# One tile of scores ahead of the last two chunks of values, with a buffer of its own for its exponents

## The chip, the cores and the metric

The kernel runs on one core of one Trainium2 chip. The metric is the time of one execution on the device in microseconds (us). The profile shows one execution; its span runs from the first to the last instruction of the program.

## The reference

Attention with pooled queries, then a small expert layer on 128 tokens of each batch. There are 8 batches, 8 heads, 1152 keys and values of 64 elements, and 576 pooled queries, all in fp32.

```
q_pool = q.reshape(B, H, S // 2, 2, D).mean(axis=3)
scores = scale * matmul(q_pool, k.T)            # scale = 1/sqrt(D)
attn   = exp(scores - max) / sum                # softmax over the keys
x      = matmul(attn, v), heads side by side    # (8, 576, 512)
for each batch b:
    top = the 128 rows with the highest x[b] @ w_gate
    out[b, top] = x[b, top] + sigmoid(score) * (relu(x[b, top] @ w1) @ w2)
```

## The kernel before

**Units of work.** Two heads make a pair; there are 32 pairs. The 576 queries of a pair are cut into two halves of 288, called s = 0 and s = 1, so the main loop in `run` goes over 64 halves, h = 0 to 63. The 1152 keys are cut into 9 chunks of 128 (NC = 9).

**Scores.** For every chunk, `scores` takes a tile from `banks()` and runs four products of 64 by 64 by 288 into it (L887; the trace has eight matmul records for the four fp32 products). ScalarE then takes the exponent of the whole tile, 128 x 576, into the SBUF tile `p` (L894). `p` holds nine such units and has two buffers, so the exponents of half h go where those of half h-2 were.

**Values.** `weighted` multiplies the exponents with the values, nine chunks one after the other, all summed in one tile of `banks()`, called `av` (L905). ScalarE copies that tile to `two` (L913), GpSimd adds its two planes (L915), and VectorE transposes the sum (L984).

**The order in a round of the loop.** In round h the program issues: the nine score tiles of half h and their exponents, small ScalarE copies for sums of earlier halves (L956 or L971), pieces of the expert layer that are due ("mid"), the sums of the exponents of half h (`folded`: three additions on GpSimd, L926, and two transposing reductions on VectorE, L931), the preparation of the next pair's keys and queries (`prepare_pair`, only where s = 0), the values of half h-1 and their copy `two`, and at the end more pieces of the expert layer. Every engine works through its instructions in this order.

**PSUM.** All matmul outputs come from one pool of four tiles, each of two banks:

```
self.psum = pool("psum", 4, space=psum)
def banks(self):
    return self.psum.tile([P, 2, 512], F32, name="ps")
```

The tiles are given out in turn. A request takes the tile given out four requests earlier and waits until its reader on ScalarE is done with it. Between two halves without a piece of the expert layer, the requests in order are: nine score tiles of half h, `av` of half h-1, nine score tiles of half h+1, and so on.

**Keys and queries of the next pair.** `load_pair` issues the transfers of keys and queries on SP's queue (L750, L756). `prepare_pair` adds neighbouring queries on GpSimd (`qp`, L775), transposes the keys on VectorE (`kT`, L778) and then the pooled queries (`qT`, L782). The scores of the next pair need both. The very first pair is prepared differently, with transposes on TensorE (`load_first`, `first_keys`, `first_queries`).

**Expert layer.** Batches are handled in twos by `layers_of_two`; its matmuls are L1362 with copies at L1370, and its activation is L1403. A search of the chosen rows runs on VectorE (L1201). What is left at the end is done in `ending` (L1439, L1449).

Semaphores are placed by the framework from the order of the program and what each instruction reads and writes. An instruction that waits for two engines has a separate EVENT_SEMAPHORE instruction ahead of it on its sequencer.

Of the kernel before, what the change touches and what calls it, by code (L numbers as in the profile page):

```python
# [10 lines left out]
P = 128  # L11
BLK = 32

G = 3
F32 = mybir.dt.float32
I32 = mybir.dt.int32
AF = mybir.ActivationFunctionType
ALU = mybir.AluOpType
# [14 lines left out]
def _any_scores(  # L33
# [451 lines left out]
    in_pair = [(j, t) for j in range(2) for t in range(NF)] + [(0, NF)]  # L485
    upcoming = load_pair(*pairs[0])
    run(prepare_pair(upcoming))
    preparing = iter(())
    routing = iter(())
# [50 lines left out]
class _Plain:  # L540
# [243 lines left out]
    def load_first(self, b, hp):  # L784


        nc, NC, D = self.nc, self.NC, self.D
        room = self.work.tile([P, self.NG, G, 2, self.HALF], F32, name="p")
        room = room.rearrange("p g u j n -> p (g u j n)")
        sixth, n_k = self.QB // 6, 2 * NC * D  # L790
        kn = room[:, 0:n_k].rearrange("p (c j d) -> p c j d", c=NC, j=2)
        n_q = 2 * 4 * sixth * D
        qn = room[0 : 3 * BLK, n_k : n_k + n_q].rearrange("p (a j m d) -> p a j m d", a=2, j=2, d=D)
        qp = room[0 : 3 * BLK, n_k + n_q : n_k + n_q + n_q // 2]
        qp = qp.rearrange("p (a n j d) -> p a n j d", a=2, j=2, d=D)
        v_sb = self.load.tile([P, 2, NC, D], F32, name="v_sb", bufs=2)
        heads = [2 * hp, 2 * hp + 1]
        of = self.q[b, 2 * hp : 2 * hp + 2].rearrange("j (i t m) d -> t i j (m d)", i=BLK, t=6)

        def queries(engine, half, groups):  # L800

            for g in groups:
                engine.dma_start(  # L803
                    qn[g * BLK : (g + 1) * BLK, half].rearrange("i j m d -> i j (m d)"), of[3 * half + g]
                )

        def keys(a, z):

            for j, h in enumerate(heads):
                rows = self.k[b, h].rearrange("(p c) d -> p c d", c=NC)  # L810
                nc.sync.dma_start(kn[:, a:z, j, :], rows[:, a:z, :])  # L811

        queries(nc.scalar, 0, (0, 1))
        queries(nc.sync, 0, (2,))
        for a in range(0, NC, G):
            keys(a, a + G)
        queries(nc.sync, 1, range(3))
        for j, h in enumerate(heads):
            of = self.v[b, h].rearrange("(p c) d -> p c d", c=NC)
            nc.sync.dma_start(v_sb[:, j, :, :], of)  # L820
        return {"k": kn, "q": qn, "qp": qp, "v": v_sb, "b": b, "hp": hp}
# [45 lines left out]
        self.first_keys(pair, 0, 1, self.nc.scalar.copy)  # L867
        self.first_keys(pair, 1, G, self.nc.vector.tensor_copy)

    def scores(self, half):  # L870

        nc, pair, n = self.nc, half["pair"], self.HALF
        qs = slice(half["s"] * n, (half["s"] + 1) * n)
        p = half["p"] = self.work.tile([P, self.NG, G, 2, n], F32, name="p")
        for c in range(self.NC):
            if "qp" in pair and half["s"] == 0:
                if c in (G - 1, G):
                    a = G * (c - G + 2)
                    self.first_keys(pair, a, a + G, nc.vector.tensor_copy)
                elif c == 2 * G - 1:  # L880
                    self.first_queries(pair, 1)
            sc = self.banks()
            for e in range(2):
                keys = slice(e * self.D, (e + 1) * self.D)
                for j in range(2):
                    rows = slice(j * self.D, (j + 1) * self.D)
                    nc.tensor.matmul(  # L887
                        sc[keys, j, 0:n],
                        lhsT=pair["kT"][rows, c * P + keys.start : c * P + keys.stop],
                        rhs=pair["qT"][rows, qs],  # L890
                        start=True,
                        stop=True,
                    )
            nc.scalar.activation(p[:, c // G, c % G, :, :], sc[:, :, 0:n], AF.Exp, scale=self.scale)  # L894

    def weighted(self, half):


        nc, n = self.nc, self.HALF
        av = self.banks()  # L900
        for c in range(self.NC):
            for e in range(2):
                keys = slice(e * self.D, (e + 1) * self.D)
                for j in range(2):
                    nc.tensor.matmul(  # L905
                        av[j * self.D : (j + 1) * self.D, e, 0:n],
                        lhsT=half["pair"]["v"][keys, j, c, :],
                        rhs=half["p"][keys, c // G, c % G, j, :],
                        start=(c == 0),
                        stop=(c == self.NC - 1),  # L910
                    )
        two = self.small.tile([P, 2, n], F32, name="two", bufs=2)
        nc.scalar.copy(two[:, :, :], av[:, :, 0:n])  # L913
        half["av"] = self.small.tile([P, n], F32, name="av", bufs=2)
        nc.gpsimd.tensor_tensor(  # L915
            out=half["av"][:, :], in0=two[:, 0, :], in1=two[:, 1, :], op=ALU.add
        )

    def folded(self, half):


        nc, nb, p, pair = self.nc, 2 * self.HB, half["p"], half["pair"]
        acc = self.work.tile([P, G, 2 * self.HALF], F32, name="acc")
        units = p.rearrange("p g u j n -> p g u (j n)")
        for u in range(G):
            nc.gpsimd.tensor_tensor(  # L926
                out=acc[:, u, :], in0=units[:, 0, u, :], in1=units[:, 1, u, :], op=ALU.add
            )
        fold = self.small.tile([P, 2, G * nb], F32, name="fold", bufs=2)
        for a, of in enumerate((units[:, 2, :, :], acc[:, :, :])):  # L930
            nc.vector.tensor_reduce(  # L931
                fold[:, a, :],
                of.rearrange("p u (m d) -> p (u m) d", d=BLK),
                AX.X,
                ALU.add,
                apply_transpose=True,
            )
        if half["s"] == 0:
            pair["sum"] = self.small.tile([P, 2, self.QB], F32, name="sum", bufs=3)
        ns = slice(half["s"] * self.HB, (half["s"] + 1) * self.HB)  # L940
        nc.vector.tensor_reduce(  # L941
            pair["sum"][:, :, ns],
            fold.rearrange("p a (u j n) -> p j n (a u)", j=2, n=self.HB),
            AX.X,
            ALU.add,
        )
# [583 lines left out]
    def ending(self, halves, old):  # L1530


        nc, half, copy, add = self.nc, self.Dm // 2, self.nc.scalar.copy, self.add
# [6 lines left out]

        tokens, a, s = self.left
        w = tokens[0]["w"]
        self.room = self.row(self.work.tile([P, self.NG, G, 2, self.HALF], F32, name="p"))
        acc = [self.row(self.work.tile([P, G, 2 * self.HALF], F32, name="acc"))]
        tiles = [self.ffn.tile([P, self.NFC, P], F32, name="hT") for _ in tokens]
        c = self.quarters_of(tiles, w)
        *m, kept = self.lines_in(acc[0], 4, w, 3)
# [24 lines left out]
        pieces(new, 1)  # L1572
        pieces(layer, 2)

        acc.append(self.row(self.work.tile([P, G, 2 * self.HALF], F32, name="acc")))
        y1, y2, y7, y3, y4 = (acc[1][0:w, i * half : (i + 1) * half] for i in range(5))
        room = self.ffn.tile([P, 4, 512], F32, name="s", bufs=1).rearrange("p a n -> p (a n)")
        s = self.lines_in(room, self.NFC // 2, w, 4)
# [1 line left out]
        for to in (y1, y2):  # L1580
            copy(to, next(second))

        room = self.row(self.work.tile([P, self.NG, G, 2, self.HALF], F32, name="p"))
        n = self.NFC * P
        tiles = [self.lines_of(room[:, i * n : (i + 1) * n]) for i in range(2)]
        of_tiles = self.quarters_of(tiles, w)
# [1 line left out]
        a = self.quarters_of(xeT, w)  # L1588
# [36 lines left out]
        s = self.lines_in(room[:, 2 * n :], self.NFC // 2, w, 4)  # L1625
# [80 lines left out]
    def run(self):  # L1706
        nc = self.nc
        pairs = [(b, hp) for b in range(self.B) for hp in range(self.NPAIR)]
        n_halves = 2 * len(pairs)
        halves = []  # L1710
        self.routing, self.behind_keys, self.last_tokens = [], [], []
        upcoming = self.load_first(*pairs[0])
        self.first_constants()
# [7 lines left out]
        for h in range(n_halves):  # L1721
            n, s = divmod(h, 2)
            if s == 0:
                pair = upcoming
# [16 lines left out]
            if 5 < h < 14 or 18 < h < 23:  # L1741
                for _ in range(2 - s):
                    next(sums, None)
            half = {"pair": pair, "s": s}
            halves.append(half)
            self.scores(half)
            if h > 1:

                of = halves[h - 2 - s]["pair"]
# [16 lines left out]
            if s == 0 and loaded:  # L1766
                upcoming = loaded
                self.prepare_pair(upcoming)
            if h > 0:
                self.weighted(halves[h - 1])  # L1770
                self.drained(halves[h - 1])
            if h > 2 and s == 1:
                self.normalized(halves[h - 2]["pair"])
# [73 lines left out]
```

## Time and profile before

| what | value |
|---|---|
| time, median of 3 runs | 680.89 us (680.37 to 681.49) |
| the profiled execution: its time | 679.94 us |
| the profiled execution: its span | 678.1 us |
| granted TensorE clock, mean | 0.999 |
| busy, of the span: PE / PEld / DVE / ACT / POOL | 99 / 66 / 84 / 67 / 75 % |
| matmul lines L887 and L905, busy | 293.1 and 291.4 us |
| exponents L894 | 576 of 693 ns |
| copy `two` L913 | 64 of 639 ns |

PE is TensorE's matmuls and PEld its weight loads, DVE is VectorE, ACT ScalarE, POOL GpSimd, SP the engine that only issues transfers. A row of the costliest groups shows the line, the engine, the operation, what it writes and reads, the number of instructions, then the busy time in us and the mean of one in ns, then the idle time of the engine just before these instructions and what ended it. The ends of matmuls in the records are modelled, their starts are not. The profiled execution's time stands 1.8 us above its span, and 0.95 us below the median of the runs.

### The profile page before, as it was taken

The numbers are of one execution on the slowest core, as the hardware profiler recorded it, in microseconds if no ns is written. First come the engines' busy times: TensorE is split into PE (matmuls) and PEld (weight loads), VectorE is DVE, ScalarE is ACT, GpSimd is POOL, SyncE is SP. The second block draws the span as 40 slices with busy tenths as digits, with TensorE's granted clock in tenths as the row PEclk, the third lists the DMA queues.
The fourth block names the chain that finished last, engine by engine and source line by source line (L and its number), as shares of the span: only waits on it lengthen the run. The fifth ranks groups of instructions, "written<-read, shape, count | busy, mean of one in ns | idle before, by whom it ended". The sixth has DMA issues, their size and how long they took to land.

```text
span 678.1 us, 23427 instructions
## 1 busy us (share of the span) xinstructions
PE 670.2 (99%) x9950; PEld 445.9 (66%) x9950; DVE 571.3 (84%) x815; ACT 454.1 (67%) x990; POOL 507.1 (75%) x477
## 2 busy tenths in 40 slices
PE   8999999999999999999999999999999999999996
PEld 5666666665666568676666657767666665657895
DVE  4878898998999887686998987676899998798974
ACT  6677777777877773855777778483777777774320
POOL 5888888889888984865897898384889889886011
PEclk9999999999999999999999999999999999999999
DMA  7888888959896785653888798474589888635211
GB/s 163 168 183 191 219 178 191 174 96 195 193 189 120 157 172 97 198 104 74 202 161 200 139 185 160 101 178 88 108 199 205 166 162 170 139 88 162 58 47 36
DMA packets 391817, 101.99 MB, mean 150 GB/s; under 512 B 371608, under 2 KB 375576, under 8 KB 390680
## 3 DMA queue, kind: packets, MB, share of 16 engines
q1 hardware_dynamic: 390264, 96.03, 67.8%
q0 software_dynamic: 1280, 4.20, 1.7%
q8 instruction: 79, 1.29, 0.8%
q14 instruction: 34, 0.28, 0.1%
q10 hardware_dynamic: 160, 0.20, 0.1%
HBM read 82.77 MB, written 17.62 MB: 148 GB/s over the span
## 4 chain that ended last, share of the span: by engine, by line
PE 93%; SPq 2%; issue 2%; DMA 1%; DVE 1%; POOL 0%; ACT 0%; POOLq 0%; DVEq 0%
PE ps L905 41%; PE ps L887 40%; PE ps L1362 7%; PE ps L1439 2%; PE ps L1449 2%; SPq L750 1%; DMA qb<-in_q_dram 1%; SPq L756 0%; SPq L811 0%; DMA out_dram<-xe,index 0%; DMA out_dram<-lines,index 0%; SPq L803 0%; DVE p L1528 0%; DVE pick L1664 0%; POOL qp L775 0%
## 5 line engine op out<-in xcount | busy, mean ns | idle before, releaser
L894 ACT ACTIVATE p<-ps 128x576 f32<-128x576 f32 x576 | 320.8, 693 | 2.9 <-PE ps L887 2.7
L926 POOL TENSOR_TENSOR acc<-p 128x576 f32<-128x576 f32 x192 | 280.6, 1490 | 25.1 <-ACT p L894 24.7
L887 PE MATMUL ps<-qT,kT 64*64 64x288 f32 x4608 | 293.1, 404 | 0.3
L905 PE MATMUL ps<-p,v_sb 64*64 64x288 f32 x4608 | 291.4, 403 | 0.0
L887 PEld LDWEIGHTS ps<-qT,kT 64*64 64x64 f32 x4608 | 173.4, 132 | 107.4 <-ACT p L894 19.3
L905 PEld LDWEIGHTS ps<-p,v_sb 64*64 64x64 f32 x4608 | 173.5, 133 | 106.2 <-ACT p L894 14.1
L931 DVE TRANSPOSE_TENSOR_REDUCE fold<-p 128x54 f32<-128x1728 f32 x64 | 126.2, 1971 | 34.9 <-ACT p L894 34.7
L931 DVE TRANSPOSE_TENSOR_REDUCE fold<-acc 128x54 f32<-128x1728 f32 x64 | 124.7, 1949 | 12.4 <-POOL acc L926 12.3
L913 ACT COPY two<-ps 128x576 f32<-128x576 f32 x64 | 40.9, 639 | 136.8 <-PE ps L905 134.3
L915 POOL TENSOR_TENSOR av<-two 128x288 f32<-128x288 f32 x64 | 51.8, 810 | 69.6 <-ACT two L913 69.5
L778 DVE STREAM_TRANSPOSE kT<-kb 128x1152 f32<-128x1152 f32 x31 | 73.3, 2363 | 0.0
L994 POOL TENSOR_TENSOR prod<-avb,w_gate 128x288 f32<-128x288 f32 x64 | 52.3, 818 | 1.1 <-DVE red L1052 0.9
L1130 DVE TENSOR_SCALAR_CACHE_REDUCE pick<-line 128x127 f32<-128x127 f32 (+4 forms) x80 | 45.2, 565 | 3.9 <-DMA line<-gate_lines 1.6
L775 POOL TENSOR_TENSOR qp<-qb 128x576 f32<-128x576 f32 x31 | 43.8, 1414 | 5.6 <-DMA qb<-in_q_dram 4.6
L984 DVE STREAM_TRANSPOSE avb<-av 128x288 f32<-128x288 f32 x64 | 28.6, 446 | 19.0 <-POOL av L915 19.0
L971 ACT ACTIVATE sums<-total,tiny 32x18 f32<-32x18 f32 x124 | 38.2, 308 | 1.9
L1030 POOL TENSOR_TENSOR x<-avb,rec 128x576 f32<-128x576 f32 x30 | 34.8, 1160 | 0.0
L956 ACT COPY groups<-sum 32x36 f32<-32x36 f32 x124 | 27.0, 218 | 2.7 <-DVE sum L941 1.2
L1052 DVE TENSOR_REDUCE red<-prod 128x9 f32<-128x288 f32 x64 | 27.9, 435 | 0.1
L941 DVE TENSOR_REDUCE sum<-fold 128x18 f32<-128x108 f32 x64 | 21.8, 341 | 2.2
L782 DVE STREAM_TRANSPOSE qT<-qp 128x576 f32<-128x576 f32 x31 | 22.9, 740 | 0.6 <-POOL qp L775 0.6
L1370 ACT COPY hT<-ps 128x512 f32<-128x512 f32 (+1 forms) x12 | 6.0, 516 | 20.7 <-PE ps L1362 20.7
(169 smaller groups left out, 444.9 us busy)
## 6 DMA issues: line engine op xcount, KB each, us to landing
kb<-in_k_dram SPq DMA_DIRECT2D x124, 144.0 KB, 4.2
qb<-in_q_dram SPq DMA_DIRECT2D x124, 144.0 KB, 3.9
v_sb<-in_v_dram SPq DMA_DIRECT2D x31, 576.0 KB, 5.7
out_dram<-x SPq DMA_DIRECT2D x128, 72.0 KB, 4.5
tw<-tw SPq DMA_DIRECT2D x8, 1024.0 KB, 6.3
lines<-row_rank SPq DMA_DIRECT2D x7, 640.0 KB, 3.7
w<-in_moe_w_dram SPq DMA_DIRECT2D x8, 512.0 KB, 4.9
tw<-tw SPq DMA_DIRECT2D x8, 512.0 KB, 5.0
```

The lines of the kernel that those rows point to most:

```text
L775: nc.gpsimd.tensor_tensor(out=qp[:, :, :], in0=pair["q"][:, :, 0, :], in1=pair["q"][:, :, 1, :], op=ALU.add)
L778: nc.vector.transpose(kT.rearrange("p (c i g) -> p c g i", c=self.NC, i=BLK), pair["k"].rearrange("p (g c) d -> p c g d", c=self.NC),)
L887: nc.tensor.matmul(sc[keys, j, 0:n], lhsT=pair["kT"][rows, c * P + keys.start : c * P + keys.stop], rhs=pair["qT"][rows, qs], start=True, ...
L894: nc.scalar.activation(p[:, c // G, c % G, :, :], sc[:, :, 0:n], AF.Exp, scale=self.scale)
L905: nc.tensor.matmul(av[j * self.D : (j + 1) * self.D, e, 0:n], lhsT=half["pair"]["v"][keys, j, c, :], rhs=half["p"][keys, c // G, c % G, j, :],
L913: nc.scalar.copy(two[:, :, :], av[:, :, 0:n])
L915: nc.gpsimd.tensor_tensor(out=half["av"][:, :], in0=two[:, 0, :], in1=two[:, 1, :], op=ALU.add)
L926: nc.gpsimd.tensor_tensor(out=acc[:, u, :], in0=units[:, 0, u, :], in1=units[:, 1, u, :], op=ALU.add)
L931: nc.vector.tensor_reduce(fold[:, a, :], of.rearrange("p u (m d) -> p (u m) d", d=BLK), AX.X, ALU.add, apply_transpose=True,)
L994: self.nc.gpsimd.tensor_tensor(out=pair["prod"][:, ns, :], in0=pair["avb"][:, ns, :], in1=self.w_gate[:, hp : hp + 1, :].broadcast_to([P, ...
L1130: nc.vector.tensor_scalar(out=cmp[0:rows, 0 : part.stop - part.start], in0=near[0:rows, part], scalar1=sc[0:rows, t : t + 1], scalar2=None ...
L1362: nc.tensor.matmul(args[0], lhsT=args[1], rhs=args[2], start=k == 0, stop=k == n - 1)
```

## The change

The unit of chunk 0 leaves `p`, which now has eight units, and goes to a tile of its own, `first`, with two buffers like `p`. `scores` takes the list of chunks to do. `weighted` of half h-1, in round h, calls `scores(following, (0,))` before its chunk 7: score tile 0 of half h+1 and its exponent now stand between chunk 6 and chunks 7 and 8 of the values of half h-1. The next round does chunks 1 to 8 only. This happens in rounds 1 to 62; half 0 and half 1 still start in their own rounds, and round 63 and `ending` have no following half. On ScalarE the exponent of tile 0 of half h+1 now stands ahead of the copy `two` of half h-1. Where the following half belongs to the next pair (s = 1 in round h), tile 0 reads that pair's `kT` and `qT`. No matmul, activation, copy or transfer is added or taken away.

The diff, without the places that only follow the new shapes of `p` and `acc`:

```diff
-    def scores(self, half):
+    def exponents_room(self):
+        return self.work.tile([P, self.NC - 1, 2, self.HALF], F32, name="p")
+
+    def exponents(self, half, c):
+        return half["p"][:, c - 1] if c else half["first"]
+
+    def scores(self, half, chunks):
...
-        p = half["p"] = self.work.tile([P, self.NG, G, 2, n], F32, name="p")
-        for c in range(self.NC):
+        for c in chunks:
+            if c == 0:
+                half["first"] = self.work.tile([P, 2, n], F32, name="first")
+            elif c == 1:
+                half["p"] = self.exponents_room()
...
-            nc.scalar.activation(p[:, c // G, c % G, :, :], sc[:, :, 0:n], AF.Exp, scale=self.scale)
+            nc.scalar.activation(self.exponents(half, c), sc[:, :, 0:n], AF.Exp, scale=self.scale)
...
-    def weighted(self, half):
+    def weighted(self, half, following=None):
...
         for c in range(self.NC):
+            if following and c == self.NC - 2:
+                self.scores(following, (0,))
...
-                        rhs=half["p"][keys, c // G, c % G, j, :],
+                        rhs=self.exponents(half, c)[keys, j, :],
...
             nc.gpsimd.tensor_tensor(
-                out=acc[:, u, :], in0=units[:, 0, u, :], in1=units[:, 1, u, :], op=ALU.add
+                out=acc[:, u], in0=self.exponents(half, u), in1=self.exponents(half, G + u), op=ALU.add
             )
...
-        halves = []
+        halves, following = [], None
...
-            half = {"pair": pair, "s": s}
+            half = following or {"pair": pair, "s": s}
             halves.append(half)
-            self.scores(half)
+            self.scores(half, range(self.NC)[1 if following else 0 :])
...
+            following = None
             if h > 0:
-                self.weighted(halves[h - 1])
+                if h + 1 < n_halves:
+                    following = {"pair": upcoming if s else pair, "s": 1 - s}
+                self.weighted(halves[h - 1], following)
```

More of the change, by code (lines that the diff above doesn't have):

```diff
@@ L787, in load_first @@
         nc, NC, D = self.nc, self.NC, self.D
-        room = self.work.tile([P, self.NG, G, 2, self.HALF], F32, name="p")
-        room = room.rearrange("p g u j n -> p (g u j n)")
+        room = self.row(self.exponents_room())
         sixth, n_k = self.QB // 6, 2 * NC * D
@@ L919, in folded @@
     def folded(self, half):
-        nc, nb, p, pair = self.nc, 2 * self.HB, half["p"], half["pair"]
-        acc = self.work.tile([P, G, 2 * self.HALF], F32, name="acc")
-        units = p.rearrange("p g u j n -> p g u (j n)")
+        nc, nb, pair = self.nc, 2 * self.HB, half["pair"]
+        acc = self.work.tile([P, G, 2, self.HALF], F32, name="acc")
         for u in range(G):
             nc.gpsimd.tensor_tensor(
-                out=acc[:, u, :], in0=units[:, 0, u, :], in1=units[:, 1, u, :], op=ALU.add
+                out=acc[:, u], in0=self.exponents(half, u), in1=self.exponents(half, G + u), op=ALU.add
             )
         fold = self.small.tile([P, 2, G * nb], F32, name="fold", bufs=2)
-        for a, of in enumerate((units[:, 2, :, :], acc[:, :, :])):
+        for a, of in enumerate((half["p"][:, 2 * G - 1 :], acc)):
             nc.vector.tensor_reduce(
                 fold[:, a, :],
-                of.rearrange("p u (m d) -> p (u m) d", d=BLK),
+                of.rearrange("p u j n -> p (u j n)").rearrange("p (m d) -> p m d", d=BLK),
                 AX.X,
@@ L1542, in ending @@
         w = tokens[0]["w"]
-        self.room = self.row(self.work.tile([P, self.NG, G, 2, self.HALF], F32, name="p"))
-        acc = [self.row(self.work.tile([P, G, 2 * self.HALF], F32, name="acc"))]
+        self.room = self.row(self.exponents_room())
+        acc = [self.row(self.work.tile([P, G, 2, self.HALF], F32, name="acc"))]
         tiles = [self.ffn.tile([P, self.NFC, P], F32, name="hT") for _ in tokens]
@@ L1573, in ending @@
         pieces(layer, 2)
-        acc.append(self.row(self.work.tile([P, G, 2 * self.HALF], F32, name="acc")))
+        acc.append(self.row(self.work.tile([P, G, 2, self.HALF], F32, name="acc")))
         y1, y2, y7, y3, y4 = (acc[1][0:w, i * half : (i + 1) * half] for i in range(5))
@@ L1581, in ending @@
             copy(to, next(second))
-        room = self.row(self.work.tile([P, self.NG, G, 2, self.HALF], F32, name="p"))
+        room = self.row(self.exponents_room())
         n = self.NFC * P
```

## The prediction

> **What bounds the kernel now.** I read the page first, then the waits of PE and PEld, then the chain of waits in order of time, then the timeline engine by engine around one boundary between two halves.
>
> ```profile
> span 678.1 us, 23427 instructions
> PE 670.2 (99%) x9950; PEld 445.9 (66%) x9950; DVE 571.3 (84%) x815; ACT 454.1 (67%) x990; POOL 507.1 (75%) x477
> PE 93%; SPq 2%; issue 2%; DMA 1%; DVE 1%; POOL 0%; ACT 0%; POOLq 0%; DVEq 0%
> L913 ACT COPY two<-ps 128x576 f32<-128x576 f32 x64 | 40.9, 639 | 136.8 <-PE ps L905 134.3
> ```
>
> The chain of waits that ended last is 93% PE and 0% ACT. It lists the same piece again and again, 4.37 us for the 72 matmul records of nine chunks, so a chunk takes 0.485 us. TensorE is full and its work does not change. So the change can win only what PE loses now: I add up how far the pieces of L887 and L905 after 30 us exceed 4.37 us in the timeline of PE (for instance 4.75 + 4.42 at 397 us, 4.56 + 4.42 at 39 us). Nine halves lose 2.0 us together to late exponents, and four boundaries to expert matmuls (L1362) lose 0.11 us each, 0.4 us in all. ScalarE idles 2.1 us per half ahead of `two`; that is cover, not cost.
>
> Now one boundary, first PE, then ACT, then what one line says of `two`'s readers:
>
> ```profile
> 109.11 4.54 PE L887 MATMUL ps<-qT,kT 64*64 64x288 f32 x72
> 113.47 4.54 PE L905 MATMUL ps<-p,v_sb 64*64 64x288 f32 x72
> ```
> ```profile
> 109.41 0.64 ACT L913 COPY two<-ps 128x576 f32<-128x576 f32 x1 [1.02 <-PE ps L905]
> 109.95 5.00 ACT L894 ACTIVATE p<-ps 128x576 f32<-128x576 f32 x9
> ```
> ```profile
> L913 ACTq EVENT_SEMAPHORE  x62: 17/17/17, 39.3 to 620.0; - x62
> ...
>   PEld ps L887: 0.2, 1
> ```
>
> The values end and the next scores start at 109.11. `two` starts 0.30 us after that and lasts 0.64, so it ends at +0.94. PE was held up by `two` once in the whole run, for a weight load that hid it. 62 of the 64 copies carry a second wait.
>
> **What the skill says.** "Perfetto Trace Analysis", section "Identifying Dependency Chains": an instruction that waits for several engines may have an EventSemaphore ahead of it. The trace agrees (62 of 64); the records to the nanosecond put such a copy 78 ns after PE's release, the two without it 23 ns after. The same page, "Tensor Engine Instruction": a matmul's end is estimated, its semaphore comes after PSUM's acknowledgement. Agrees: PE's release of `av` is recorded 0.22 us after the next phase has begun. "TensorE: Matmul & The Clock Gate", section "Step-by-step: what each phase is for": weight loads are pulled ahead of matmuls in flight, so a late one can be hidden. Agrees: L887's loads waited 86 times for exponents, most of them without moving a matmul.
>
> **How late a weight load may be.** An exponent's end to the weight load that waited for it is 0.05 us (398.25 + 0.65 = 398.90, load at 398.95). Where load and matmul start together, that matmul lasts 453 ns instead of 402 and its chunk is 0.05 us longer. So a chunk is on time only if its bank is released 0.10 us before its start.
>
> **The change part by part.**
>
> *Moved matmuls, exponent, copies.* The same 4 products, 576 exponents and 64 copies remain. The switch between score and value matmuls costs nothing now (chunks keep 0.485 us across 109.11 and 113.47), and two more switches per half are taken at nothing; 0 to 0.02 us each by the restart cost if a load is late. The early exponent runs in ScalarE's idle time: its tile is done 0.75 us before the values' last release, one exponent occupies ACT 0.54 us. No DMA moves; SP's queue is not passed. POOL's first addition reads `first` and chunk 3, which come 0.5 us earlier, nothing waits longer. Taken at 0.
>
> *The new wait.* PSUM has four tiles. Score tile 3 of the next half takes over `av`'s tile, before and after. Before, tiles 0 to 2 stand between the end of the values and tile 3: it starts at +1.455 us (3 x 0.485) and `two` needs to end by +1.35; it ends at +0.94. After, only tiles 1 and 2 stand between: tile 3 starts at +0.97, its load can go at 0.94 + 0.05 = +0.99. Lateness 0.02, plus the 0.05 of the restart: **0.073 us of TensorE per half**. What is queued behind it is everything on PE. `two` itself can't come earlier, because it waits for the last value chunk. This holds in 61 rounds (2 to 62; in round 1 `two` has a single wait, 0.02 us): 61 x 0.073 + 0.02 = **+4.5 us**. Unknown: whether `two` keeps two waits. The early exponent has waited for POOL already, so that wait of `two` can go, but then its own buffer's last write is a wait left over; I keep two. With one, 0.055 less: 0.018 per half, +1.1 us. Below that it would need 0.02 more luck, so the lower end is 0; the upper end is +5.5, if the copy is some 15 ns slower behind an exponent.
>
> *Queries needed earlier.* Tile 0 of a new pair is issued 0.97 us (two chunks) earlier and PE, in order, holds chunks 7 and 8 behind it. In the 31 pairs `qT` is ready 2.2 us or more ahead, except in three:
>
> ```profile
> 20.57 0.78 DVE L782 STREAM_TRANSPOSE qT<-qp 128x576 f32<-128x576 f32 x1 [0.61 <-POOL qp L775]
> 21.47 0.96 PEld L887 LDWEIGHTS ps<-qT,kT 64*64 64x64 f32 x20 [0.62 <-issue]
> 21.50 1.20 PE L887 MATMUL ps<-qT,kT 64*64 64x288 f32 x16
> ```
> ```profile
> 343.52 0.74 DVE L782 STREAM_TRANSPOSE qT<-qp 128x576 f32<-128x576 f32 x1
> ```
> ```profile
> 344.53 4.54 PE L887 MATMUL ps<-qT,kT 64*64 64x288 f32 x72
> ```
>
> The first: `qT` ends at 21.35 and sets the start at 21.50, which costs 0.31 us now. Chunk 7 of those values would start at 16.78 + 0.52 + 6 x 0.485 = 20.21, so PE waits 1.29 us there: **+1.0 us**. `qT` hangs on `qp`, and that on a transfer, so it can't come sooner. The second (344 us): ready at 344.26 + 0.15, wanted at 344.53 - 0.97 = 343.56, 0.85 us late. The third (510 us; `qT` 508.99 to 509.74, scores at 510.19) is 0.67 us late. DVE is busy without a gap there since 315 us, where its last idle was 0.28; with that and the delay that PE itself has gathered (some 0.25) I take 0.35 and 0.15: **+0.5 us**, between 0.2 and 1.5.
>
> *ReLU rounds.* In two rounds L1403 (2.00 us at 278.08) ends 0.43 us past the values; `two` starts at +0.34 instead of +0.30. After, exponent 0 stands between. The exponents end 0.59 earlier, so L1403 ends at -0.16 and `two` starts at about +0.35: **+0.1 us**. Without that cover, 0.5 each.
>
> *Waits taken away.* After the change `av`'s tile is released by exponent 5, which follows `two` by one exponent less. Its load comes at +3.72, the chunk is due at 8 x 0.485 + 0.07 = +3.95; the slack beyond the 0.05 grows from 0.05 to 0.18 us. So each late half saves up to 0.13 where the delay is on an exponent, nothing where it is on `two` itself (39.6 and 607.0 us, 0.3 late each, which now hit tile 3 directly): **-0.6 us**, 0 to -1.3. The expert matmuls' first bank comes from the same exponent: **-0.4 us**, 0 to -0.4.
>
> Sum: 4.5 + 1.0 + 0.5 + 0.1 - 0.6 - 0.4 = +5.1 us. The profiled execution's 679.94 (span 678.1 and 1.8 around it) becomes 685.0; the median stands 0.95 above that execution, so the prediction is 680.89 + 5.1 = **686.0 us**.
>
> **Rivals.** *A, the forecast*: PE waits for `two` in every half; 684.0 to 688.2. For it: TensorE has no slack and the releases are read off the same trace. Chance 0.76.
>
> *B, a single wait on `two`*: 1.1 instead of 4.5, everything else as above: +1.7, 682.6 us; 681.5 to 684. For it: the wait on POOL is indeed met earlier. Against: 62 of 64 copies show two waits. Chance 0.14.
>
> *C, not slower: the lead does what it looks like.* If `two`'s release reaches tile 3's load 0.073 us sooner than I reckon (end at +0.87 or earlier), PE never waits there. With all late halves cured, 2.0 + 0.4 us go, and the queries of the first pair give 1.0 to 1.5 back: 680.0 us, 678.5 if the queries come in time as well. The deciding point is one: the start of `two`, +0.23 or +0.30 after the values. For it: PE's idle shows 2 us of waits on ACT. Against: the 0.30 repeats in all undisturbed halves. Chance 0.10. That the edit changes nothing at all is excluded: three score tiles become two ahead of a fixed copy.
>
> **How the numbers follow.** A measurement of this kernel tells about 0.2%, 1.4 us, from no change: slower is above 682.3, faster below 679.5. A is slower throughout, B in some two thirds, C is within 0.2% in half of its cases and faster in the rest: slower 0.85, same 0.10, faster 0.05. The range reaches from B's centre to A's high end (new wait 5.5, queries 1.0 + 1.5, nothing won back): 682.4 to 688.2.
>
> **What would show it.** Right: in the waits of PEld a row L887 waiting for `two`, some 60 times; between the values and the ninth score chunk a period of 8.80 instead of 8.73 us per half; at about 20.2 us a PE gap of 1.3 us in the middle of the values; ACT idle ahead of `two` shorter by an exponent. The step on the new wait is wrong if that row is missing or `two` starts 0.245 us past the values; the step on the queries is wrong if PE doesn't stop in the values near 20, 343 and 509 us. The whole is wrong if the period stays at 8.73 us.

## The result, and the profile after

The changed kernel takes 683.23 us in the median (681.23 to 684.19), the kernel before, beside it, 680.37 us (679.71 to 682.05): the ratio over all executions is 1.0026, with a 95% interval of 1.0016 to 1.0036. The forecast was 686.0. So the change is slower, as forecast, but by less than the forecast's 5.1 us: 1.8 us (1.1 to 2.4) by that ratio, 2.1 between the means, 2.9 between the medians. The times of a kernel lie in groups, and a median jumps from one to the other; where the start is alike (last experiment) the medians are 2.0 us apart. None of this comes from the mechanism that carried the forecast.

The lines of the changed kernel: scores L895 (before L887), exponents L902 (L894), values L915 (L905), `two` L923 (L913), sums on GpSimd L935 (L926) and VectorE L940 (L931), `groups` L965 (L956), `total` L971 (L962), `sums` L980 (L971), expert matmuls L1371 (L1362). First the page: span, busy times, the shares of the chain that ended last, and `two`.

```profile
span 679.4 us, 23510 instructions
...
PE 669.9 (99%) x9950; PEld 475.9 (70%) x9950; DVE 574.3 (85%) x815; ACT 460.2 (68%) x990; POOL 506.5 (75%) x477
...
PE 83%; DVE 10%; DMA 2%; issue 2%; ACT 1%; POOL 1%; ACTq 0%; SPq 0%; DVEq 0%; POOLq 0%
...
L923 ACT COPY two<-ps 128x576 f32<-128x576 f32 x64 | 40.8, 638 | 24.8 <-PE ps L915 24.8
```

The profiled execution took 681.23 us (before: 679.94). It is the fastest of the 11, so what the slower ones lose beyond it is in no trace. PE's share of the chain fell from 93 to 83% and VectorE's rose from 1 to 10%: somewhere PE now waits for VectorE. ACT idles 0.4 us ahead of each `two` instead of 2.1, since the early exponent stands there. Now the boundary between two halves that the prediction showed, PE first, then ACT:

```profile
108.10 0.69 PE L895 MATMUL ps<-qT,kT 64*64 64x288 f32 x8
108.58 1.18 PE L915 MATMUL ps<-p,v_sb 64*64 64x288 f32 x16
109.56 4.09 PE L895 MATMUL ps<-qT,kT 64*64 64x288 f32 x64
```
```profile
108.91 0.65 ACT L902 ACTIVATE first<-ps 128x576 f32<-128x576 f32 x1 [0.59 <-PE ps L895]
109.88 0.64 ACT L923 COPY two<-ps 128x576 f32<-128x576 f32 x1 [0.32 <-PE ps L915]
110.42 4.46 ACT L902 ACTIVATE p<-ps 128x576 f32<-128x576 f32 x8
```

`two` starts 0.32 us after the values' end and ends at +0.96, near the forecast's +0.94. But score tile 3, due at +0.97, isn't late. Its first weight load is this one:

```profile
110.28 0.13 PEld L895 LDWEIGHTS ps<-qT,kT 64*64 64x64 f32 x1
```

It starts 0.24 us before `two` ends (109.88 + 0.64 = 110.52), and in all 62 rounds with an early tile this load comes 0.18 to 0.27 us before the end of `two`. So tile 3 cannot be waiting for `two`. The eight tiles of scores after 109.56 run on in one piece at 0.485 us each (113.44 - 109.56 = 3.88 = 8 x 0.485), and the period of a half stays at 8.73 us (the median of 61), which the prediction had named as its sign of being wrong as a whole. All that is said of `two`:

```profile
L923 ACTq EVENT_SEMAPHORE  x62: 17/17/17, 40.0 to 621.0; - x62
...
  POOL av L925: 84.1, 34
```

62 of the 64 copies still carry two waits, and of PEld, which stood here once before, there is no row: PE never waits for `two`. What PE does wait for stands in its timeline at three places in the middle of the values, and the chain of waits says why:

```profile
20.78 0.71 PE L895 MATMUL ps<-qT,kT 64*64 64x288 f32 x8 [0.31 <-DVE qT L782]
...
344.26 0.71 PE L895 MATMUL ps<-qT,kT 64*64 64x288 f32 x8 [0.68 <-DVE qT L782]
...
510.46 0.71 PE L895 MATMUL ps<-qT,kT 64*64 64x288 f32 x8 [0.55 <-DVE qT L782]
```
```profile
336.69 3.75 DVE fold L940 x2
...
341.29 2.23 DVE kT L778
343.53 0.60 DVE qT L782
344.12 0.14 issue
344.26 0.71 PE ps L895 x8
```

In each, the early tile of the new pair stands still for `qT`, and chunks 7 and 8 of the values behind it. At 344 us VectorE comes to `qT` only after both sums of the exponents and the keys.

**Where PE's time goes.** In each trace I took the starts of consecutive chunks on PE, subtracted 0.485 us and sorted the rest by its place and what the weight load waited for. Seven of the traces, in us; "start" is up to 19.7 us (in the third row up to 22), "switches" are the borders with expert matmuls:

| trace | start | `qT` | late exponents | `two` | switches | sum |
|---|---|---|---|---|---|---|
| before | 0.68 | 0.34 | 2.00 | 0 | 0.76 | 3.79 |
| changed | 0.60 | 2.15 | 1.13 | 0 | 0.75 | 4.63 |
| changed, tiles in turn | 2.02 | 2.14 | 0 | 4.54 | 0.75 | 9.46 |
| changed, not into three pairs | 0.61 | 0 | 1.29 | 0 | 0.76 | 2.65 |
| changed, once more | 0.61 | 2.43 | 0 | 0 | 0.84 | 3.87 |
| before, ten products | 0.60 | 0 | 2.47 | 0 | 0.76 | 3.83 |
| changed, ten products | 0.61 | 2.17 | 1.78 | 0 | 0.75 | 5.31 |

The first two rows tell the story of the change: `qT` +1.81, late exponents -0.87, `two` nothing. The other rows are the experiments below. They ran on several chips, each beside the kernel before on its own chip, whose median is given with each.

### The profile page after: what moved, and what is told of

Its sections match the earlier page's. It is cut to its first block, busy times and chain, and to the rows that moved or that the text cites. A ratio compares the mean times of both kernels' runs of the same rounds, so it can differ in the third digit from the quotient of the medians.

```text
span 679.4 us, 23510 instructions
## 1 busy us (share of the span) xinstructions
PE 669.9 (99%) x9950; PEld 475.9 (70%) x9950; DVE 574.3 (85%) x815; ACT 460.2 (68%) x990; POOL 506.5 (75%) x477
## 3 DMA queue, kind: packets, MB, share of 16 engines
q8 instruction: 79, 1.29, 0.8%
## 4 chain that ended last, share of the span: by engine, by line
PE 83%; DVE 10%; DMA 2%; issue 2%; ACT 1%; POOL 1%; ACTq 0%; SPq 0%; DVEq 0%; POOLq 0%
PE ps L915 36%; PE ps L895 36%; PE ps L1371 7%; DVE fold L940 3%; PE ps L1448 2%; DVE pick L1210 2%; DVE kT L778 2%; PE ps L1458 2%; DMA kb<-in_k_dram 1%; DMA row_rank<-both 0%; DMA p<-in_q_dram 0%; DVE qT L782 0%; DMA out_dram<-xe,index 0%; DMA out_dram<-lines,index 0%; DVE xe L1462 0%
## 5 line engine op out<-in xcount | busy, mean ns | idle before, releaser
L895 PE MATMUL ps<-qT,kT 64*64 64x288 f32 x4608 | 305.2, 403 | 1.7 <-DVE qT L782 1.5
L902 ACT ACTIVATE p<-ps 128x576 f32<-128x576 f32 x512 | 286.0, 691 | 2.0 <-PE ps L895 2.0
L915 PE MATMUL ps<-p,v_sb 64*64 64x288 f32 x4096 | 272.7, 402 | 0.0
L895 PEld LDWEIGHTS ps<-qT,kT 64*64 64x64 f32 x4608 | 188.2, 133 | 93.8 <-ACT p L902 6.4
L915 PEld LDWEIGHTS ps<-p,v_sb 64*64 64x64 f32 x4096 | 170.0, 133 | 78.3
L935 POOL TENSOR_TENSOR acc<-p 128x576 f32<-128x576 f32 x128 | 189.6, 1501 | 0.0
L940 DVE TRANSPOSE_TENSOR_REDUCE fold<-p 128x54 f32<-128x1728 f32 x64 | 126.1, 1971 | 29.0 <-ACT p L902 28.6
L940 DVE TRANSPOSE_TENSOR_REDUCE fold<-acc 128x54 f32<-128x1728 f32 x64 | 124.7, 1949 | 13.7 <-POOL acc L935 13.6
L902 ACT ACTIVATE first<-ps 128x576 f32<-128x576 f32 x64 | 41.6, 650 | 107.3 <-PE ps L895 103.3
L935 POOL TENSOR_TENSOR acc<-first,p 128x576 f32<-128x576 f32 x64 | 93.6, 1462 | 16.1 <-ACT p L902 16.0
L923 ACT COPY two<-ps 128x576 f32<-128x576 f32 x64 | 40.8, 638 | 24.8 <-PE ps L915 24.8
L915 PE MATMUL ps<-first,v_sb 64*64 64x288 f32 x512 | 43.9, 406 | 0.0
L980 ACT ACTIVATE sums<-total,tiny 32x18 f32<-32x18 f32 x124 | 38.2, 308 | 2.0
L965 ACT COPY groups<-sum 32x36 f32<-32x36 f32 x124 | 27.1, 219 | 2.7 <-DVE sum L950 1.3
```

The source lines that it names most:

```text
L895: nc.tensor.matmul(sc[keys, j, 0:n], lhsT=pair["kT"][rows, c * P + keys.start : c * P + keys.stop], rhs=pair["qT"][rows, qs], start=True, ...
L902: nc.scalar.activation(self.exponents(half, c), sc[:, :, 0:n], AF.Exp, scale=self.scale)
L915: nc.tensor.matmul(av[j * self.D : (j + 1) * self.D, e, 0:n], lhsT=half["pair"]["v"][keys, j, c, :], rhs=self.exponents(half, c)[keys, j, ...
L935: nc.gpsimd.tensor_tensor(out=acc[:, u], in0=self.exponents(half, u), in1=self.exponents(half, G + u), op=ALU.add)
L940: nc.vector.tensor_reduce(fold[:, a, :], of.rearrange("p u j n -> p (u j n)").rearrange("p (m d) -> p m d", d=BLK), AX.X, ALU.add, apply_t ...
```

## The experiments

**My theory after the result.** The wait for `two` isn't missing because it was cheap, but because score tile 3 takes another tile than I had thought. I take it that the pool hands out first the tile that ScalarE releases first, and ScalarE does the early exponent ahead of `two`: then tile 3 takes the early tile's own room, and tile 4 that of `two`. The weight loads fit this: that of tile 3 comes before the end of `two`, that of tile 4 in all 62 rounds 0.21 to 0.30 us after it. So `two` still has until +1.455 - 0.10 us. What is lost is the early need of `qT` (theory Q). Rivals: the wait would be hidden at +0.97 us anyway (H), or something is lost in every half (S).

### Tiles in turn

```diff
-        return self.psum.tile([P, 2, 512], F32, name="ps")
+        self.given = getattr(self, "given", -1) + 1
+        return self.psum.tile([P, 2, 512], F32, name=f"ps{self.given % 4}", bufs=1)
```

> The change, with the four PSUM tiles given out strictly in turn, so that score tile 3 takes the tile of `av` and waits for `two`, and tile 4 waits for nothing. Theory R (the forecast's price was right for a wait that the changed kernel doesn't have, because there the pool hands out first what ScalarE releases first, the tile of the early exponent): PE waits for `two` in 61 halves, 0.07 to 0.09 us each, so 4.5 to 5.5 us above the changed kernel, 6 to 8 above the kernel before. Theory H (the wait on `two` at +0.97 us would have been hidden by the weight load anyway): within 0.5 us of the changed kernel, no row of PEld waiting for `two`.

Measured: 685.73 us (684.70 to 686.66), before 680.5; ratio 1.0077, interval 1.0060 to 1.0095. In the waits of PEld the row that I had forecast is there, with all its halves; below it one `two` and the load of tile 3 behind it:

```profile
PEld ps L895 <- ACT two L923: 21.7, 62, 0.4
```
```profile
112.78 0.64 ACT L923 COPY two<-ps 128x576 f32<-128x576 f32 x1 [0.31 <-PE ps L915]
```
```profile
113.47 2.63 PEld L895 LDWEIGHTS ps<-qT,kT 64*64 64x64 f32 x48 [0.35 <-ACT two L923]
```

In all 62 halves the load of tile 3 now comes 0.05 us after the end of `two`. As a rule tile 3 then starts 0.024 us late and its chunk is 0.051 us longer: 0.075 us, a period of 8.805 us, and 4.54 us together in the table, where the prediction had 0.073, 8.80 and 4.5. R's wait and its price hold, H falls. The time missed R's figure: it is 5.2 us above the kernel before, not 6 to 8, and the changed kernel didn't run on this chip. One reason is that the late exponents are gone, so that against the changed kernel's trace (without the start) the net is +3.4 us; that they go because PE gives ScalarE 0.075 us more per half is my reading, not shown. The wait that the forecast priced belongs to a program whose tiles go strictly in turn. That this kernel's time lands next to 686.0 is in part chance, since the smaller terms of the forecast don't have these sizes.

### Without an early tile into the three pairs with late queries

```diff
-                if h + 1 < n_halves:
+                if h + 1 < n_halves and h + 1 not in (2, 36, 52):
```

> The change, but without an early tile in front of halves 2, 36 and 52, the three whose queries are late. Theory Q (what the change costs is the early need of queries in three pairs, and nothing else is lost): the stops in the values at 20.8, 344.3 and 510.5 us (0.49 + 0.86 + 0.73 us in the trace of the changed kernel) go, 0.32 at 21.5 us comes back; loss of PE on chunks 4.63 - 1.76 = 2.9 us against 3.79 of the kernel before, so 0.5 to 0.9 us below the kernel before, ratio 0.9987 to 0.9993. Theory S (a cost spread over all halves, by the copy, the switches between score and value matmuls, or the wait on `two`): the time stays 1 us or more above the kernel before.

Measured: 680.23 us (678.93 to 681.52), before 680.5; ratio 0.9997, interval 0.9986 to 1.0008. The scores of half 36 follow the values without a wait (PE's timeline):

```profile
341.62 2.60 PE L915 MATMUL ps<-p,v_sb 64*64 64x288 f32 x40
344.05 2.35 PE L895 MATMUL ps<-qT,kT 64*64 64x288 f32 x34
```

All of the loss against the kernel before is gone with three of 62 early tiles, so S falls. The sum of PE's losses is 2.65 us, 1.1 below that of the kernel before. Of the gain that Q expected, 0.5 to 0.9 us, the median shows 0.3, inside its own uncertainty, so a gain over the kernel before isn't shown.

### One chunk, three chunks

The edit with one chunk; with three it is `NC - 3`.

```diff
-            if following and c == self.NC - 2:
+            if following and c == self.NC - 1:
```

> The early tile stands in front of one chunk of values instead of two. Theory Q: the queries are wanted 0.485 us later, so the stops at 344.3 and 510.5 us shrink from 0.86 and 0.73 to 0.37 and 0.25 us, the one at 20.8 us by 0 to 0.49; all else as in the changed kernel, late exponents too: 1.0 to 1.5 us below the changed kernel. Theory S (cost in every half): within 0.4 us of the changed kernel.

> The early tile stands in front of three chunks of values instead of two. Theory Q (the cost is how early the queries are wanted): the stops at 344.3 and 510.5 us grow from 0.86 and 0.73 by 0.2 to 0.485 each, the first from 0.5 by up to 0.485; 0.6 to 1.5 us above the changed kernel. Theory P (the position as such costs nothing): within 0.3 us.

Measured, one chunk: 680.79 us, before 680.5, ratio 1.0013 (1.0002 to 1.0023). Three chunks: 683.48, before 678.54, ratio 1.0063 (1.0049 to 1.0076). PE at half 36, first with one chunk, then with three:

```profile
344.52 0.71 PE L895 MATMUL ps<-qT,kT 64*64 64x288 f32 x8 [0.34 <-DVE qT L782]
```
```profile
345.95 0.71 PE L895 MATMUL ps<-qT,kT 64*64 64x288 f32 x8 [1.23 <-DVE qT L782]
```

By the starts of the chunks the stops at halves 36 and 52 are 0.52 and 0.56 us with one chunk, 0.86 and 0.73 with two, 1.41 and 1.40 with three: the further ahead the tile, the longer PE stands. The step isn't a clean 0.485 us each time, since `qT` itself came 0.25 us later in the trace with one chunk; there I had expected 0.37 and 0.25. The stop at the first pair doesn't follow (0.59, 0.49 and 1.00 us); those queries hang on a transfer. In time, three chunks take 0.8 us more than the changed kernel on the same chip (682.65, below), as expected. With one chunk I had expected 1.0 to 1.5 us less than the changed kernel, which didn't run on that chip; by the two ratios to the kernel before (1.0026 and 1.0013) it is 0.9. Q holds in its direction and roughly in its size.

### The buffer alone

```diff
-                if h + 1 < n_halves:
+                if False:
```

> Only the tile of its own for chunk 0's exponents; the order of all work as in the kernel before. Theory Q: same as the kernel before within 0.3 us, late exponents at the same places with the same 2.0 us of TensorE. Rival: the finer tile lets exponent 0 start sooner or later (its buffer is released by one addition on GpSimd instead of by the last reduction), and a share of the 0.9 us that the changed kernel won on late exponents shows here: 0.3 to 0.9 us below the kernel before.

Measured: 679.97 us, before 680.5; ratio 0.9996 (0.9985 to 1.0008). No difference is shown. The trace has 1.35 us of late exponents, against 2.00 and 2.47 in the traces of the kernel before with eight and with ten products, so a gain of the rival's smaller size isn't excluded. On this same chip the kernels with an early tile have 1.12 (one chunk) and 1.29 (not into three pairs): how much of the -0.87 is owed to the early tile, and how much to the buffer, is open.

### Queries ahead of the sums

```diff
+            if h in (34, 50):
+                self.prepare_pair(loaded)
             self.folded(half)
...
-                self.prepare_pair(upcoming)
+                if h not in (34, 50):
+                    self.prepare_pair(upcoming)
...
-                if h + 1 < n_halves:
+                if h + 1 < n_halves and h + 1 != 2:
```

> The early tile stands everywhere except into half 2; in rounds 34 and 50 the keys and queries of the next pair are prepared ahead of the sums of the half's exponents instead of behind them (same instructions, other order on VectorE and GpSimd). Theory D (the stops at 344.3 and 510.5 us are VectorE's order: queries stand behind 4 us of sums): both stops go, time as without an early tile into these pairs, 0.3 to 0.9 us below the kernel before. Rival T (the queries hang on a transfer or on GpSimd): stops stay at 0.3 us or more each, time 0.6 us or more above that.

Measured: 687.0 us (684.13 to 687.68), before 678.54; ratio 1.0120 (1.0103 to 1.0137). Both stops for `qT` are gone (PE's early tile starts at 342.60 without a wait), so they were indeed VectorE's order. But the expectation missed the time by about 9 us. ScalarE's timeline shows the reason:

```profile
337.77 2.86 ACT L902 ACTIVATE p<-ps 128x576 f32<-128x576 f32 x5
344.87 1.27 ACT L980 ACTIVATE sums<-total,tiny 32x18 f32<-32x18 f32 x4 [4.25 <-DVE total L971]
346.17 0.85 ACT L965 COPY groups<-line 32x18 f32<-32x18 f32 x4
346.93 0.63 ACT L902 ACTIVATE first<-ps 128x576 f32<-128x576 f32 x1
347.47 0.61 ACT L923 COPY two<-ps 128x576 f32<-128x576 f32 x1
```

`total` (L971) now comes 3.9 us later on VectorE (344.46, against 340.58 in the changed kernel on the same chip), ScalarE works in order and waits 4.25 us for it, and the exponent of the early tile and `two` stand behind. PE runs out of tiles for 2.6 us ahead of 347.61, and again ahead of 515.70: here late sums cost more than late queries. These two stops are 5.2 of the 5.6 us by which the profiled execution (684.13, the shortest of the five) stands above the kernel before. The other four, near 687, have a granted clock of 0.995 instead of 0.999; whether their further 3 us come from that isn't in this trace.

### Two early tiles

```diff
-                self.scores(following, (0,))
+                self.scores(following, (0, 1))
...
-        return half["p"][:, c - 1] if c else half["first"]
+        return half["p"][:, c - 2] if c > 1 else half["first"][:, c]
...
-                if h + 1 < n_halves:
+                if h + 1 < n_halves and h + 1 not in (2, 36, 52):
...
```

> Score tiles 0 and 1 of the next half both stand in front of the last two chunks of values, with one tile of two units for their exponents; not into halves 2, 36 and 52; one scratch block of the ending moves to that tile. Theory L (ScalarE's cadence of 0.53 us per exponent against 0.485 us per chunk makes the late exponents, and each exponent that is out of the way before `two` gives 0.13 us of slack): the late exponents that were left with one early tile (1.29 us in the trace of the kernel with one early tile outside those three pairs) go down to 0 to 0.3, so 0.9 to 1.3 us below that kernel, some 1.3 to 2 us below the kernel before. Rival: `two` now queues behind two exponents and comes later, or the two weight loads more per half cost: 0 to 2 us above the kernel with one early tile.

Measured: 679.68 us (679.31 to 681.66), before 678.54; ratio 1.0018 (1.0010 to 1.0026). Slower, which theory L had not expected. Late exponents are down to 0.14 us, but the changed kernel on the same chip has none either (row "once more"), so there was nothing to win here. And halves 36 and 52, which have no early tile, now wait for `qT`, 0.44 and 0.46 us. PE in this trace, then `two` ahead of VectorE's long stretch of work, here and in the changed kernel once more on the same chip:

```profile
345.50 1.88 PE L895 MATMUL ps<-qT,kT 64*64 64x288 f32 x25 [0.26 <-DVE qT L782]
```
```profile
311.41 0.64 ACT L923 COPY two<-ps 128x576 f32<-128x576 f32 x1 [0.26 <-PE ps L915]
```
```profile
309.84 0.64 ACT L923 COPY two<-ps 128x576 f32<-128x576 f32 x1 [0.31 <-PE ps L915]
```

The second early tile moves the end of the values, and with it `two`, back by one more chunk. Where these values begin, PE is 1.09 us behind the other trace (305.72 against 304.63), and `two` 1.57: the difference is a chunk of 0.485. VectorE's stretch begins with the sum that `two` feeds and has no idle from 313 us to `qT`, which is 1.57 us behind as well (344.62 against 343.05), while PE at 344 us is still only 1.1 behind. So `qT`, which was just in time for a half without an early tile, is late by nearly a chunk. That is worked out from two traces; no run takes this delay alone away. L had looked only at ScalarE.

### The changed kernel once more, and a longer start

> The changed kernel once more, beside the others. Two of its first runs' groups are 1.5 us apart, as those of the kernel before. Expected: stops at 20.8, 344.3 and 510.5 us again, each within 0.4 us of 0.49, 0.86 and 0.73; 1.3 to 2.9 us above the kernel before. If the 2.9 us between the medians are a real cost, the sum of the stops and late exponents has to exceed that of the kernel before by that much in this trace; if they are a matter of which group was drawn, by 0.8 to 1.5.

Measured: 682.65 us (680.67 to 682.95), before 678.54; ratio 1.0049 (1.0035 to 1.0063). The stops are 0.51, 0.94 and 0.91 us: they repeat. Late exponents are absent. The time is 3.3 us above the kernel before by the ratio and 4.1 by the medians, more than the 1.3 to 2.9 expected. The trace holds 2.4 us of stops, with no late exponents for the change to win back; it is that of the fastest of six executions, and the kernel before has no trace on this chip, so the rest is open. The ScalarE waits of the kernel before (first line) and of this run (second) differ in one row:

```profile
ACT p L894 <- PE ps L887: 2.7, 8, 0.8
```
```profile
ACT p L902 <- PE ps L895: 1.1, 3, 0.5
```

Exponents waited for PE's release 6 to 8 times in the traces that have late exponents everywhere (before, changed, and both with ten products), 3 or 4 times in those of this chip. ScalarE needs 0.53 us per exponent against PE's 0.485 per chunk, so I take it that a half that begins late stays late. Why PE's releases come late only on some chips is open.

The last pair of kernels concerns the start. The products of ones (L622) keep TensorE busy before the first transposes; the edit makes ten of eight, in the kernel before, in the changed one, and in the one without an early tile into the three pairs:

```diff
-        for _ in range(8):
+        for _ in range(10):
```

> The kernel before with ten instead of eight products of ones at its very start. In some executions TensorE runs its first score tiles at a low clock until about 8.7 us (684 ns a record), in others only until 4.2 to 5.5 us (402 ns), which sets two groups of times 1.5 us apart. Theory G (the gap of 0.5 us between the last of these products and the first transpose keeps a window of the clock from counting as busy): all executions in the lower group, 0 to 0.2 us above its 679.6 us of chip 8 or 678.4 us of chip 14; median 0.3 to 1.0 us lower. Rival F (the group is a matter of the window's free phase alone): two groups as before, median within 0.3 us or up to 0.2 above.

> The changed kernel with the same ten products. Theory G: one group, at 681.2 to 681.6 us on a chip that has late exponents (1.6 us above the kernel before with ten products), or 680.7 on one that has none (2.2 above). If the changed kernel's median of 683.2 has another cause than the start, it stays above 682. Theory on late exponents: the trace of the kernel before has 2.0 us of them on a chip where this trace has 1.1, or both have none, and the difference between the two kernels is 0.9 us larger where there are none.

> Ten products at the start and no early tile into halves 2, 36 and 52. Theory G with theory Q: below the kernel before by 0.7 to 1.5 us, 0.3 to 0.9 below the kernel before with ten products on a chip with late exponents, within 0.3 of it where there are none. Rival: within 0.3 us of the kernel before.

Measured, beside a median of 680.47 us (679.35 to 682.39) of the kernel before: before with ten 680.18 (679.45 to 680.96), changed with ten 682.16 (681.69 to 682.53), not into three pairs with ten 680.01 (678.90 to 680.54). PE's start in the kernel with its own tile alone, eight products, and in the kernel before with ten:

```profile
1.04 3.78 PE L622 MATMUL ps<-ones 128*128 128x128 f32 x16 [1.04 <-POOL ones L615]
...
6.57 2.20 PE L895 MATMUL ps<-qT,kT 64*64 64x288 f32 x16
```
```profile
1.04 4.63 PE L622 MATMUL ps<-ones 128*128 128x128 f32 x20 [1.04 <-POOL ones L615]
...
6.64 1.20 PE L887 MATMUL ps<-qT,kT 64*64 64x288 f32 x16
```

With eight products some executions do their first score tiles in 2.20 us instead of 1.20 (684 ns a record instead of 402). In four of the ten traces with eight products PE's records stay at the longer times until 9.3 to 10.6 us, in the other six only until 3.9 to 5.5 us, and in the three with ten until 5.0 to 6.5 us. With ten, 22 executions of each kernel lie within 0.8 to 1.6 us of each other; the 59 of the kernel before with eight lie within 3.0. The Trainium skill ("TensorE: Matmul & The Clock Gate", section "What's actually happening") describes a clock at half rate until one window of about 3.4 us has been busy, with windows that run free of the kernel's start. The times at which the long records end agree with a rule of that kind, though the records are 1.7 times as long and not twice. Theory G holds for the scatter; its gain in the median is 0.3 us, at the low end (ratio 0.9992, 0.9986 to 0.9999). The two products fill the idle time and also lengthen the busy stretch; the runs don't tell these apart.

So with the start alike the change costs 682.16 - 680.18 = **2.0 us**, by the medians (1.8 by the two ratios). I had expected 1.6 on a chip with late exponents, and 682.16 lies just above the 682 that I had named as the sign of another cause than the start; so by that sign the draw of the start isn't the whole cause of the first median, 683.23, and the rest is open. Of these 2.0 us the three early tiles account for all: with ten products the changed kernel stands 682.16 - 680.01 = 2.15 us above the kernel without them, and its trace has 2.17 us of stops for `qT`. That third kernel has a ratio of 0.9986 (0.9979 to 0.9993) to the kernel before, so it beats it, by 1.0 us (0.5 by the medians), in good part by its start. Against the kernel before with ten products 0.4 us are left by the ratios and 0.17 by the medians, less than these runs can tell; by the ratios both figures are as expected, by the medians both fall short.

## Why the prediction was right in direction and wrong in its main step

**The new wait, +4.5 us: this step failed.** It rested on "Score tile 3 of the next half takes over `av`'s tile, before and after". "After" is false, and so is the sentence ahead of the prediction that a request takes the tile given out four requests earlier; before the change the order of release and the order of requests are the same, and the trace couldn't tell them apart. Moving the exponent ahead of `two` swapped the order of release, tile 3 got the early tile's own room, and `two` kept its 0.4 us of slack. Measured: 0 us, with tile 3's load ahead of the end of `two` in all 62 rounds. The price was right: 4.54 us where the tiles go in turn. The rule that the pool goes by the order of release is inferred from these two kernels; that tile 3 doesn't wait for `two` is shown.

**A single wait (rival B), 14%.** Also not what happened: the EVENT_SEMAPHORE stands 62 times, and `two` starts at +0.32. B's 682.6 was nearer to the result for another reason. **Rival C's deciding point**, the start of `two` at +0.23 or +0.30, decided nothing, since tile 3 doesn't wait for it.

**Queries, +1.0 and +0.5 us.** The sum is near (+1.8 and, in the second trace, +2.1 with the 0.34 of before taken off), the parts aren't. The raw readings of lateness, 0.85 and 0.67 us, were right: 0.86 and 0.73. At 344 us that is in part luck: VectorE's stretch began 0.30 us later, since `two` comes a chunk later, and won 0.54 back on one instruction (L1462, before L1453, at 313 us: 1.09 us instead of 1.64). What failed is the allowance that took them down to 0.35 and 0.15. There VectorE was earlier by 0.14 us and not by 0.28, and PE, which I had thought 0.25 us later, came 0.16 us earlier, because it lost less to late exponents on the way. At the first pair +1.0 was too much: `qp` began at 18.37 us instead of 19.13, its transfer having landed sooner in this execution, and the stop was 0.49 us instead of 1.29.

**Late exponents, -0.6 us.** Measured -0.87, and -0.7 with ten products (1.78 against 2.47); within the 0 to -1.3 given, though the early tile's part in it is open (see "The buffer alone"). **Expert matmuls, -0.4 us.** Measured 0: the 0.110 us at each of these borders isn't ScalarE's. It stays in the changed kernel, and in the kernel with two early tiles, whose exponents come half a microsecond sooner. I had taken the releaser that the row names for the cause. **ReLU rounds, +0.1:** nothing shows at 278 us.

With the first term at zero, 1.0 + 0.5 + 0.1 - 0.6 - 0.4 gives +0.6 us, too little to be told from no change; so the right direction is owed to queries that cost more, and expert matmuls that won less, than forecast. The true sizes of the rest give 1.81 - 0.87 - 0.08 (start) = +0.86 in the chunks of the first two traces. The profiled executions differ by 1.29; the other 0.4 lie outside of these chunks (0.1 of it ahead of the first), and weren't followed up. The ends of the forecast's range don't follow from its own terms: 680.89 + 5.5 + 1.0 + 1.5 + 0.1 is 689.0 and not 688.2, and B's centre is 682.6 and not 682.4.

## What to carry to other kernels

Before a wait is priced on a rotating buffer, find out which buffer the request really gets: a move that changes the order of releases can change the order of the buffers, and with it who waits for whom. A lead for one step makes every input of that step due earlier by the same lead; list the inputs with the least slack, and take the raw lateness as the price unless a run shows the allowance. Where a lead costs only in a few rounds, leave it out there first: three of 62 early tiles held all of the loss.

## What the runs showed of the hardware that was not expected

- From 64 by 64 products to full-array ones PE loses 0.110 us at each border, no matter when the exponents come, and 0.051 on the way back (four borders in the loop, one in the ending; single ones at 0.139).
- Late exponents take 2.0 to 2.5 us of TensorE in the traces of the kernel before with eight and with ten products; on the chip where the changed kernel's trace has none, the kernel before ran at 678.5 us instead of 680.5.
- Two products more in an idle half microsecond at the very start took 1.5 us of scatter away.
- VectorE's product for `xe` (L1462, before L1453), with two inputs of 128 x 512, lasts 1.09, 1.63 or 1.91 us, and in all 13 traces (26 instances) it starts during one of GpSimd's additions (L935, before L926) and ends 0.55 us after that addition. The Trainium skill ("SBUF — State Buffer", section "SBUF: two separate sides") says that VectorE with two inputs in SBUF and a GpSimd instruction that reads SBUF lock the same pair of ports for a whole instruction, and the later one waits; the traces agree, but no run takes the overlap alone away.
